# Slot lists loaded apart from their adding, expert weights put behind them, and writes of out without waits on one another

## The chip, the cores and the metric

One Trainium2 chip, of which the kernel uses one core. The metric is the device time of an execution in microseconds. The engines: PE (TensorE, matrix products and transposes), ACT (ScalarE), DVE (VectorE), POOL (GpSimd), and SP (SyncE), which here only issues DMAs and loads registers. Each engine works through its own stream in order and waits on semaphores. DMAs issued by SP and those issued by POOL go through different queues.

## What is computed

An attention with a window of 128, a mixing stage (two Fourier transforms, real part) with a dense feed-forward block, and a routed mixture of experts: 2304 tokens of 512 numbers, 8 experts with 1024 hidden units. The change touches only the last of the three. Cut to that:

```python
logits = np.einsum('bsd,de->bse', x, w_gate)
local_gate = 1.0 / (1.0 + np.exp(-np.einsum('bsd,de->bse', x, w_local).squeeze(-1)))
for b in range(B):
    prev_e = -1
    for s in range(S):
        fresh_e = int(np.argmax(logits[b, s]))
        if s == 0 or local_gate[b, s] < 0.5:
            e = fresh_e
        else:
            e = prev_e if prev_e >= 0 else fresh_e
        prev_e = e
        ls = logits[b, s] - logits[b, s].max()
        p = np.exp(ls)
        p /= p.sum() + 1e-09
        h = np.maximum(x[b, s] @ w1[e], 0.0)
        out[b, s] = p[e] * (h @ w2[e])
```

## The kernel before, in words

The dense block runs in two halves over nine groups of two 128-token tiles. While its second half runs, each finished group is routed: `route` makes logits and one-hot choices, `assign` turns them into a slot for each token (a running count for each expert) and scatters an entry (token, output row, factor) for each token into the DRAM lists `slots`, three lists whose sum is the entry. The experts are then taken in an order by their counts (`ranks`, `er` holds the expert of a rank and `eb` the first slot). The rows that a rank has room for are fixed: 224, 384, 320, 320, 296, 272, 232 and 216 for ranks 0 to 7. The two fullest tiles of the first expert are done early: rank -1, called the early FFN here, 256 rows, whose expert is known before the last groups are routed. Rank 0 is the same expert and uses the same weights.

A matrix product in full precision is three products of rounded halves: `split` (lines 164 to 166) makes the high half by a cast on ACT and the rest by a subtraction on DVE, and `mm3` (lines 168 to 171) issues the three matmuls. So every weight chunk of a rank (four chunks of 1 MB, each loaded by two DMAs from SP into a raw tile, of which there are two) costs four splits, and every tile of tokens four transposes on PE and a split (`transpose_split`, line 549).

`ffn` (line 563) is a generator. For each of 8 blocks f it issues 12 hidden matmuls, a relu on ACT and a second half of the relu on DVE, and yields; from f = 1 on it then issues the products with the second weights for block g = f - 1 (six matmuls for two tiles), and yields. So there are 16 yields, n = 0 to 15: n = 0 is f=0, n = 1 is f=1, then g=0, f=2, g=1, f=3 and so on to g=7. Between yields, other generators take steps: `beside` (inputs of the next rank), `soon` (the early expert) and `pre_` (weights). `last` holds the newest hidden matmul, relu and second half of a relu; `tc.issue_after(ins)` pins instructions behind one of them on its engine, and `behind()` (line 605) pins behind all three. What isn't pinned, the framework orders by itself: at build time it fills each engine's stream, in the order of the program as far as things are ready by its own estimate of times, else in another order. DMA issues on SP are ordered in the same way.

The inputs of a rank: `slot_load` (line 1118) loads the three lists, `slot_ids` (line 1124) adds them on DVE and copies the numbers out, `gather` (line 1100) fetches token rows by an indirect DMA from POOL (256 KB for a full tile), and `transpose_split` brings them into the form that the FFN reads. `early` (line 1137) does the same for the early FFN, in the dense block's last group: after the gathers it lets EY steps pass (5) and then transposes. `expert_inputs` (line 1212) does it for ranks 0 to 7, with `slot_load` and `slot_ids` in one step. In the early FFN (lines 1229 to 1240), at n = 5, expert 1's weights are queued first, then rank 0's inputs. `emit` (line 1106) scales a finished tile on ACT (or ACT and DVE) and writes its rows to `out` by an indirect DMA from POOL. Since each write may touch any row of `out`, the framework lets it wait for the one before.

## Time and profile before

| what | value |
|---|---|
| median of 3 runs | 980.01 us (977.08 to 980.98) |
| the profiled execution, its own time | 980.93 us |
| its span | 978.9 us |
| PE busy | 910.6 us (93%) |
| DVE, ACT, POOL busy | 521.8, 369.8, 239.7 us |
| early FFN | from 697.1 us on |
| FFN of rank 0 | from 736.2 us on |
| last matmul | 962.7 us |

The profiled execution is one of the program on the chip, taken by the hardware profiler. Its time lies 2.0 us above its span and 0.9 us above the median. Times in rows count from the span's start. In a timeline a row is: start, duration (both us), engine, line, operation, output<-input, shapes and a count, and in brackets how long the engine stood idle before it and what released it. A matmul's duration overlaps with the next; the distance of starts tells its cost. A line can be that of a helper: L169 to L171 are the three matmuls of `mm3`, L165 and L166 the two halves of `split`, L552 the transposes, L580 and L583 the relu and its second half. The name `hps` is a hidden block's result, `acc` the output's, `tps` a transposed tile, `we` raw weights, `xg` gathered rows, `ids` the lists, `idn` the slot numbers, `yo` a finished tile.

### The profile page before, as it was taken

How to read it: one execution, taken by the hardware profiler on the slowest of the kernel's cores; microseconds unless marked ns; L12 is line 12 of the kernel's file. 1: busy time of each engine (PE TensorE's matmuls, PEld its weight loads, DVE VectorE, ACT ScalarE, POOL GpSimd, SP SyncE). 2: the span in 40 equal slices, each digit the busy share in tenths (PEclk: the TensorE clock that was granted, in tenths of full speed). 3: DMA queues.
4: the chain of work that ended last, by engine and by line, in shares of the span. 5: the costliest groups of instructions: out<-in, count | busy, mean ns of one | idle time of the engine just before them, and what ended most of it. 6: DMA issues, size and time to landing. Idle time of an engine off the chain costs nothing. (4 is left out here: it accounts for less than half of the span.)

```text
span 978.9 us, 16130 instructions
## 1 busy us (share of the span) xinstructions
PE 910.6 (93%) x5878; PEld 752.2 (77%) x5879; DVE 521.8 (53%) x1332; ACT 369.8 (38%) x974; POOL 239.7 (24%) x364
## 2 busy tenths in 40 slices
PE   8868899989999999999999999998979999999993
PEld 4535677667778797889888888887758899988782
DVE  5787866745554658521333435357546545565410
ACT  5635363543553246421111111114235445455410
POOL 2315441231221137310111313123023211222100
PEclk9989799979999999999999999999988999999997
DMA  9923071341312396253444342536167555455100
GB/s 324 378 86 108 1 238 61 121 130 52 114 66 69 120 313 194 65 151 65 108 108 108 85 110 44 120 85 194 57 188 247 186 162 164 165 189 196 64 20 20
DMA packets 109036, 129.14 MB, mean 132 GB/s; under 512 B 16222, under 2 KB 78046, under 8 KB 108884
## 3 DMA queue, kind: packets, MB, share of 16 engines
q1 hardware_dynamic: 83636, 103.95, 33.3%
q0 software_dynamic: 22720, 19.36, 9.1%
q10 hardware_dynamic: 2592, 4.72, 1.3%
q8 instruction: 48, 0.79, 0.3%
q14 instruction: 40, 0.33, 0.1%
HBM read 99.65 MB, written 30.87 MB: 133 GB/s over the span
## 5 line engine op out<-in xcount | busy, mean ns | idle before, releaser
L580 ACT ACTIVATE h<-hps 128x256 fp32r<-128x256 f32 x152 | 58.2, 383 | 262.3 <-PE hps L171 259.0
L583 DVE SCALAR_TENSOR_TENSOR h<-hps,h 128x256 fp32r<-128x256 f32 x152 | 63.8, 420 | 160.0 <-ACT h L580 160.0
L169 PE MATMUL acc<-t,h 128*128 128x512 f32 x304 | 125.8, 416 | 3.0 <-ACT h L580 3.0
L171 PE MATMUL acc<-t,h 128*128 128x512 f32 x304 | 121.7, 400 | 1.5 <-DVE h L583 1.2
L170 PE MATMUL acc<-t,h 128*128 128x512 f32 x304 | 121.9, 401 | 1.0 <-POOL t L166 0.9
L166 DVE TENSOR_TENSOR t<-we,t 128x512 fp32r<-128x512 f32 x128 | 84.5, 694 | 46.9 <-ACT t L165 46.9
L169 PE MATMUL hps<-xT,t 128*128 128x256 f32 x288 | 87.0, 302 | 4.8 <-ACT t L165 3.5
L165 ACT CAST t<-we 128x512 fp32r<-128x512 f32 x128 | 73.4, 618 | 42.4 <-DMA we<-in_w 17.9
L171 PE MATMUL hps<-xT,t 128*128 128x256 f32 x288 | 84.7, 294 | 3.5 <-POOL t L166 3.5
L169 PE MATMUL hps<-xTe,t 128*128 128x320 f32 (+7 forms) x288 | 86.4, 301 | 0.6 <-ACT xTe L165 0.6
L170 PE MATMUL hps<-xTe,t 128*128 128x320 f32 (+7 forms) x288 | 86.0, 299 | 0.0
L171 PE MATMUL hps<-xTe,t 128*128 128x320 f32 (+7 forms) x288 | 85.8, 298 | 0.0
L170 PE MATMUL hps<-xT,t 128*128 128x256 f32 x288 | 83.9, 291 | 0.0
L169 PE MATMUL hps<-xTb,t 128*128 128x256 f32 x288 | 83.6, 290 | 0.0
L170 PE MATMUL hps<-xTb,t 128*128 128x256 f32 x288 | 82.3, 286 | 0.0
L171 PE MATMUL hps<-xTb,t 128*128 128x256 f32 x288 | 82.3, 286 | 0.0
L378 ACT ACTIVATE t<-t,mx 128x128 f32<-128x128 f32 (+1 forms) x160 | 62.6, 393 | 45.7 <-DVE mx L371 41.3
L171 PEld LDWEIGHTS acc<-t,h 128*128 128x128 f32 x304 | 57.8, 190 | 17.9 <-DVE h L583 5.0
L169 PEld LDWEIGHTS acc<-t,h 128*128 128x128 f32 x304 | 58.1, 192 | 14.8 <-ACT h L580 3.2
L169 PEld LDWEIGHTS hps<-xT,t 128*128 128x128 f32 x288 | 56.8, 197 | 12.5 <-ACT t L165 4.4
L170 PEld LDWEIGHTS acc<-t,h 128*128 128x128 f32 x304 | 58.2, 191 | 9.8 <-POOL t L166 2.8
L583 DVE SCALAR_TENSOR_TENSOR hE<-hps,hE 128x256 fp32r<-128x256 f32 (+4 forms) x96 | 30.8, 349 | 62.6 <-ACT hE L580 62.1
(280 smaller groups left out, 2018.3 us busy)
## 6 DMA issues: line engine op xcount, KB each, us to landing
we<-in_w SPq DMA_DIRECT2D x64, 512.0 KB
rw<-in_w_ch SPq DMA_DIRECT2D x32, 512.0 KB
qkt<-in_qk SPq DMA_DIRECT2D x15, 642.0 KB
nd<-xT SPq DMA_DIRECT2D x18, 512.0 KB
xTb<-nd POOLq DMA_DIRECT2D x18, 512.0 KB, 6.8
vt<-in_v SPq DMA_DIRECT2D x16, 384.0 KB
pd<-y ACTq DMA_DIRECT2D x18, 256.0 KB
ub<-ud SPq DMA_DIRECT2D x18, 256.0 KB
```

What stands on the lines that cost most here:

```text
L165: nc.scalar.copy(hi, src)
L166: (eng or nc.vector).tensor_tensor(out=lo, in0=src, in1=hi.bitcast(F32), op=ALU.subtract)
L169: nc.tensor.matmul(o, lhsT=wh, rhs=xh, start=start, stop=False, **kw)
L170: nc.tensor.matmul(o, lhsT=wh, rhs=xl, start=False, stop=False, **kw)
L171: return nc.tensor.matmul(o, lhsT=wl, rhs=xh, start=False, stop=stop, **kw)
L378: nc.scalar.activation(t[0:m, j], t[0:m, j], AF.Exp, bias=mx[0:m, j:j + 1], scale=-1.0, accum_out=sums[0:m, j:j + 1])
L580: last["relu"] = nc.scalar.activation(h[:, 0:n], hps[:, 0:n], AF.Relu)
L583: last["rest"] = nc.vector.scalar_tensor_tensor(out=h[:, lo:lo + c1 - c0], in0=hps[:, c0:c1], scalar=0.0, in1=h[:, c0:c1].bitcast(F32), op ...
```

## The change

Four things are changed.

1. EY is 7 instead of 5: the early expert's transposes come two steps later.
2. `expert_inputs` issues the list loads, lets `apart` steps pass (5 for rank 0, 3 for the others), and only then adds the lists, behind the newest relu. Its transposes are pinned behind the newest hidden matmul. In the loop over ranks, its first step comes at n = 0 instead of n = 2, and ahead of the weights' step.
3. In the early FFN rank 0's inputs are queued first. Expert 1's weights follow once the gathers are issued: two raw chunks are loaded behind the last list load on SP, and all splits happen in rank 0's FFN, behind its relus. Behind the early FFN's last hidden block stand 12 matmuls (128x512) whose result nobody reads; rank 0's last transposes are pinned behind them.
4. A write of `out` is declared independent of the write before it, except in the block for overfull experts (`single`), which isn't entered here.

```diff
-EY = 5
+EY = 7
 EL = 7
+IL = 5
+SPIN = 12
...
-    def expert_weights(r, e):
+    def expert_weights(r, e, ahead=False):
...
-        for c in range(F // CB):
-            t1, t2 = chunksE[r][c]
+        def raw(c):
             x = act.tile([P, 2, 4 * CB], F32, tag="xT", name="we")
             x1, x2 = x[:, 0].rearrange("p (k f) -> p k f", k=4), x[:, 1].rearrange("p (k f) -> p k f", k=per)
             nc.sync.dma_start(out=x1.unsqueeze(1), in_=w1[:, bass.ds(e, 1), :, c * CB:(c + 1) * CB])
             nc.sync.dma_start(out=x2.unsqueeze(1), in_=w2[:, bass.ds(e, 1), c * per:(c + 1) * per, :])
+            return x1, x2
+
+        q = []
+        if ahead:
+            with tc.issue_after(last["ids"].ins):
+                q = [raw(0), raw(1)]
+            yield
+        for c in range(F // CB):
+            t1, t2 = chunksE[r][c]
+            x1, x2 = q.pop(0) if q else raw(c)
...
-    def emit(acc, idx, m=P, both=False):
+    def emit(acc, idx, m=P, both=False, alone=True):
...
+        if alone and wrote:
+            tc.declare_no_dep(w.ins, wrote[-1], reason="each token has one slot, so the rows are others")
+        wrote.append(w.ins)
...
-            nc.sync.dma_start(out=x[:, i, 0:nt], in_=slots[i][bass.ds(s0, nt * P)].rearrange("(t p) c -> p t c", p=P))
+            last["ids"] = nc.sync.dma_start(out=x[:, i, 0:nt], in_=slots[i][bass.ds(s0, nt * P)].rearrange("(t p) c -> p t c", p=P))
...
-    def expert_inputs(r):
+    def expert_inputs(r, apart):
         nt = -(-CAPS[r] // P)
-        ids[r] = slot_entries(eb[r], nt, NL)
+        x = slot_load(eb[r], nt, NL)
+        for _ in range(apart):
+            yield
+        with behind():
+            ids[r] = slot_ids(x, nt, NL)
...
         for t in range(nt):
-            transpose_split(xTs[r], t * P, gs[t], rows[t])
+            with tc.issue_after(last["ffn"].ins):
+                transpose_split(xTs[r], t * P, gs[t], rows[t])
             yield
...
-            pre_.add(expert_weights(1, er[1]))
-            pre_.step()
-            beside.add(expert_inputs(0))
-            beside.step(TE)
-        elif xp is not None and n < 15:
-            pre_.step(2)
+            beside.add(expert_inputs(0, IL))
+            beside.step()
+            left = IL + TM - 1
+        elif xp is not None and left:
+            left -= 1
+            beside.step()
+            if not left:
+                pre_.add(expert_weights(1, er[1], True))
+                pre_.step()
+    spin = ps_a2.tile([P, DM], F32, tag="acc2", name="spin")
+    t2 = chunksE[-1][0][1]
+    with behind():
+        for _ in range(SPIN):
+            last["ffn"] = nc.tensor.matmul(spin, lhsT=t2[:, 0, 0, 0:P], rhs=t2[:, 0, 0], start=True, stop=True)
...
-            beside.add(expert_inputs(r + 1))
+            beside.add(expert_inputs(r + 1, 3))
...
-            pre_.step(1 if r else 2)
-            if n >= 2:
-                beside.step()
+            beside.step()
+            with behind() if r == 0 else nullcontext():
+                pre_.step(1 if r else 2)
```

## Rows read from the trace of the kernel before

**Rows 1.** Busy time by stretch: PE, PEld, DVE, ACT, POOL; PE clock; DMA share; GB/s

```profile
730.00:740.00 10.00, 6.08 (x28) 5.22 (x29) 6.82 (x15) 6.74 (x13) 2.18 (x3) 0.62 0.86 249
```

**Rows 2.** PE's timeline at the early expert's transposes

```profile
687.70 0.78 PE L552 MATMUL tps<-ident,xg 128*128 128x128 f32 x4 [1.93 <-DMA xg<-x2d,idn]
...
690.83 0.90 PE L552 MATMUL tps<-ident,xg 128*128 128x128 f32 x4
...
692.97 0.28 PE L169 MATMUL hps<-xTb,t 128*128 128x256 f32 x1
...
694.39 0.40 PE L169 MATMUL acc<-t,h 128*128 128x512 f32 x1
```

**Rows 3.** PE's timeline from the early FFN to that of rank 0

```profile
721.36 0.28 PE L171 MATMUL hps<-xTe,t 128*128 128x256 f32 x1
724.67 0.50 PE L169 MATMUL acc<-t,h 128*128 128x512 f32 x1 [3.02 <-ACT h L580]
...
730.75 0.65 PE L552 MATMUL tps<-ident,xg 128*128 128x128 f32 x4 [1.72 <-DMA xg<-x2d,idn]
...
734.70 0.90 PE L552 MATMUL tps<-ident,xg 96*128 96x96 f32 x4 [2.60 <-DMA xg<-x2d,idn]
736.17 0.77 PE L169 MATMUL hps<-xTe,t 128*128 128x224 f32 x2 [0.57 <-ACT xTe L165]
...
743.48 0.26 PE L169 MATMUL hps<-xTe,t 128*128 128x224 f32 x1
...
744.81 0.40 PE L169 MATMUL acc<-t,hE 128*128 128x512 f32 x1
...
746.21 0.26 PE L169 MATMUL hps<-xTe,t 128*128 128x224 f32 x1
```

**Rows 4.** Timelines of DVE and of PE in rank 1's FFN

```profile
766.25 0.38 DVE L1128 TENSOR_TENSOR ids<-ids 128x12 f32<-128x12 f32 x2 [4.10 <-DMA ids<-slots]
...
768.66 0.50 PE L171 MATMUL acc<-t,hE 128*128 128x512 f32 x1 [1.31 <-DVE hE L583]
```

**Rows 5.** POOL's timeline behind the last matmul

```profile
963.45 1.00 POOL L1115 DMA_INDIRECT out<-yo,idn  x1 [17.20 <-ACT yo L1114]
967.50 1.00 POOL L1115 DMA_INDIRECT out<-yo,idn  x1 [3.06 <-issue]
```

**Rows 6.** POOL's timeline at the seam, and all gathers of line 1103 to landing

```profile
713.16 0.98 POOL L990 DMA_INDIRECT slots<-ent,su  x1 [0.30 <-issue]
726.48 1.35 POOL L1103 DMA_INDIRECT xg<-x2d,idn  x1 [12.34 <-ACT h L580]
728.14 1.18 POOL L1103 DMA_INDIRECT xg<-x2d,idn  x1 [0.31 <-issue]
...
DMA to landing us min/median/max: 4.4/5.1/6.5
```

**Rows 7.** Timelines of ACT and of DVE at the seam

```profile
721.56 1.14 ACT L165 CAST t<-we 128x512 fp32r<-128x512 f32 x2 [5.10 <-DMA we<-in_w]
...
725.61 0.16 DVE L1131 COPY idn<-ids 128x2 f32<-128x2 f32 x1
```

**Rows 8.** SP's DMA issues by line, 700 to 720: min/median/max ns, first to last start

```profile
L1089 SPq DMA_DIRECT2D we<-in_w x2: 372/382/393, 715.0 to 718.9; - x2
...
L1121 SPq DMA_DIRECT2D ids<-slots x3: 373/745/792, 715.6 to 717.2; - x3
```

**Rows 9.** Instructions of POOL's queue behind the last matmul, by line: min/median/max ns, starts

```profile
L1115 POOLq EVENT_SEMAPHORE  x1: 3386/3386/3386, 963.3 to 963.3; - x1
...
L1292 POOLq EVENT_SEMAPHORE  x5: 17/43/43, 970.4 to 970.8; - x5
```

**Rows 10.** Timelines of PE and of DVE in rank 2's FFN (320 rows)

```profile
806.10 0.39 PE L169 MATMUL acc<-t,hE 128*128 128x512 f32 x1
806.77 0.56 DVE L583 SCALAR_TENSOR_TENSOR hE<-hps,hE 128x256 fp32r<-128x256 f32 x2 [1.79 <-ACT hE L580]
...
809.70 0.60 PE L552 MATMUL tps<-ident,xg 128*128 128x128 f32 x4
```

More of the change, by code (lines that the diff above doesn't have):

```diff
@@ L1104, in gather @@
         return g
-    def emit(acc, idx, m=P, both=False):
+    wrote = []
+    def emit(acc, idx, m=P, both=False, alone=True):
         y = act.tile([P, DM], F32, tag="y", name="yo")
@@ L1114, in emit @@
             nc.scalar.activation(y[0:m], acc[0:m], AF.Copy, scale=idx[0:m, 2:3].bitcast(F32))
-        nc.gpsimd.indirect_dma_start(out=out, out_offset=IOA(ap=idx[0:m, 1:2], axis=0), in_=y[0:m], in_offset=None,
-                                     bounds_check=NT - 1, oob_is_err=False)
+        w = nc.gpsimd.indirect_dma_start(out=out, out_offset=IOA(ap=idx[0:m, 1:2], axis=0), in_=y[0:m], in_offset=None,
+                                         bounds_check=NT - 1, oob_is_err=False)
+        if alone and wrote:
+            tc.declare_no_dep(w.ins, wrote[-1], reason="each token has one slot, so the rows are others")
+        wrote.append(w.ins)
     def slot_load(s0, nt, lists):
@@ L1265, in single @@
                 mm3(acc, t[:, 0, f, 0:P], t[:, 1, f, 0:P], t2[:, 0, f % per], t2[:, 1, f % per], c + f == 0, c == 2 and f == 3)
-        emit(acc, idx)
+        emit(acc, idx, alone=False)
     nc.vector.tensor_single_scalar(eid[:, 0], eid[:, 0], 3, op=ALU.arith_shift_right)
```

## The prediction

> **What bounds the kernel now.** The page comes first: of the engines TensorE is busy longest by far, so a change can only pay where PE stands idle or runs at the lower clock, or behind its last matmul. The table by stretch finds the largest such place: from 730 to 740 PE is busy for 6.08 us of 10 at a granted clock of 0.62, between its two levels of 1.2 and 2.4 GHz, while the DMA engines are 0.86 busy [rows 1]. PE's timeline then names what it waits for. First, at 687.70 the early expert's first transpose waits 1.93 us for a gather, and the hidden block behind it runs at half clock until 690.83 [rows 2]. Second, the seam between the early FFN and the FFN of rank 0: from the last hidden matmul at 721.36 to the third hidden block at 743.48 there are four large waits (3.02 for a relu, 1.72 and 2.60 for gathers, 0.57 for the split after them) and two stretches at half clock [rows 3]. Third, 1.31 us at 768.66 [rows 4]. Fourth, the tail behind the last matmul, where the second write of out starts 4.05 us after the first [rows 5].
>
> The chain that makes the seam is read backwards over four engines. The gathers start at 726.48 and 728.14 [rows 6], because the slot numbers were ready at 725.77 [rows 7]; those wait for lists issued from 715.6 to 717.2, behind the first raw weights at 715.0 [rows 8]. ScalarE meanwhile sits in its in-order stream at a cast that waits for those weights until 721.56 [rows 7], and the relu behind it holds PE (the 3.02 us). So one early load, that of expert 1, is late for ACT and in the way of the lists at once.
>
> **EY from 5 to 7.** The two early transposes move behind one more acc block and one more hidden block. From 685.6 on that is hidden f=6 (1.42 us at full clock, the distance of 692.97 and 694.39 [rows 2]), acc g=5 (1.40 [rows 3]), then the first transpose at 688.4, after the landing seen at 687.70. The second follows at 690.2; that its gather has landed by then isn't seen, only that it has at 690.83 without a wait. The wait of 1.93 goes, and of the 3.13 us from 687.70 to 690.83 about 1.35 (0.36 for the transposes and 1.42 would do). Together 3.3, less 0 to 0.6 if the second gather is late: I take 3.2. The split of the second tile (some 1.3 us) ends before the early FFN starts at some 693.8, so nothing else becomes late.
>
> **The seam: IL, the weights put behind the lists, the spin.** All times here are 3.2 us earlier than in the trace. The lists depend on the last scatter into slots (713.16, now 710.0). The last of the three list loads was issued at 717.2 [rows 8], some 4 us after that scatter; now that is 714.0. How long a list takes with no weights ahead of it the trace doesn't show. Bounds: 3.3 us, by a write of out that starts at 963.45 and whose successor's wait ends at 966.7 [rows 5, 9], and some 8 us, by the same list behind a megabyte (717.2 to the slot numbers of 725.6, less the adds) [rows 7, 8]. I take 3.3, as the change puts it ahead. Slot numbers need 0.7 us on DVE (0.38 for two adds [rows 4], 0.16 for each of two copies [rows 7]) and are pinned behind the relu of f=5, which is past by then. POOL starts 0.2 to 0.7 later (725.77 to 726.48 [rows 6, 7]). First gather near 718.2, second 1.7 later at 719.9; landing 4.4 to 6.5, median 5.1 [rows 6]: second tile there at 724.3 to 726.4, say 725.1. PE ends f=7 at 718.3, and g=6 and g=7 at 721.1, as nothing stands ahead of the relus any more: the casts of expert 1's weights are pinned behind the relus of the next FFN. Twelve spin matmuls of 0.233 (1.40 for six [rows 3]) last until 723.9. They cost nothing as long as the gathers are later than that, and 2.8 us if these came at once. The transposes then wait 1.2, the split takes 1.3 more, and the FFN starts at 726.4. Before, it started at 736.17, and its first 7.31 us (to 743.48) would have taken 4.06 at full clock (two hidden blocks of 1.33 and one acc block of 1.40 [rows 3]), so the equal start is 739.4. Gain 13.0, of which 3.2 were counted: 9.8. The last idle stretch may again drop the clock, as the 1.93 us did [rows 2], at 1.35 us there and 3.25 at the seam (7.31 less 4.06); I put 0.8 on it. **Seam 9.0**, bounds 5 (gathers of 6.5 us and the clock lost) and 11.
>
> **Expert 1's weights inside rank 0's FFN.** Two raw chunks (2 MB) are issued behind the lists, two more when buffers come free. The 16 splits put 9 us on ACT (1.14 for two [rows 7]) and about as much on DVE, in an FFN of some 23 us (eight times 2.73 [rows 3], and transposes). Raws 3 and 4 leave at about 731 and 735, land some 6.5 us later (715.0 to 721.56 [rows 7, 8]) and are split by 745, 4 us before rank 1 starts and needs the first of them. The cover is that slack; without it PE would wait up to 3 us. I take 0.5. SP moves no more DMAs than before, only in another order, so later ranks start with their weights one half rank less ahead, which their length hides (28.8 us at 320 rows, eight times the 3.60 of [rows 10]).
>
> **Lists of ranks 1 to 7.** In rank 1's FFN, DVE stood 4.10 us at a list add with the relu's second half behind it, and PE lost 1.31 [rows 4]. With the add three steps after the load and behind a relu this goes: 1.3.
> But the pin has a price. Now slot numbers and gathers run almost a whole FFN ahead; then they start only after the third hidden block's relu. Take the FFN of 320 rows [rows 10]: that block ends at 806.10 (call it X), DVE starts the relu's second half at 806.77 and ends 0.56 later, the slot numbers take 0.7, POOL's start 0.2 to 0.7: the gather starts at X + 2.1 to 2.6 and lands at X + 6.5 to 9.1. The transposes stood at 809.70, after g=1 and f=3 (3.60 us); one step later, behind g=2 as well, that is X + 5.5. So **PE waits there 1.0 us by the quickest landing, 2.2 by the median and the later start, 3.6 by the slowest**; nothing of it is in the trace of before. In rank 0's FFN the place by the program is X + 4.1, in rank 1's about X + 6.3, in the last two, with two tiles, X + 3. But the order isn't only the program's. In the seam the transposes stood inside g=7, far behind their place in the program (f=3), and the slot numbers behind the relu of f=6; between lie g=5, f=7, g=6 and half of g=7, 4.8 us by [rows 3], less 1.2 for that relu. So the framework reckons some 3.6 us from slot numbers to landing, which puts the transposes at X + 5.2 or later everywhere. Bounds for seven FFNs: 0 (transposes placed later still) and 25. I take the quickest landing, **1.0 each, 7.0 in all**, because the DMA engines are less full later than in the seam.
>
> **Writes of out.** POOL no longer waits for a landing. In the middle nothing waits for POOL. In the tail the second write can start 0.3 after the first ends, at 964.75 instead of 967.50; the semaphores that close the kernel stand behind it on POOL's queue, at 970.4 to 970.8 [rows 9], and move with it; the other engines' stand earlier. **2.75**, bounds 0 and 3.
>
> Sum: 3.2 + 9.0 + 1.3 + 2.75 - 0.5 - 7.0 = 8.75. The profiled execution took 980.93 us, 2.0 more than its span; 972.2 by the sum. The median of the three runs is 0.9 below that execution, so I predict **971.3**, by itself 966 to 976.
>
> **Rivals.**
> *Gathers in time* (0.26): the transposes are placed late enough and none of the seven waits. For it: no such wait is in the trace after rank 0; against it: that trace gathers far ahead. Time 964.3.
> The Trainium skill would have it so: "DMA: Bandwidth & Descriptors", section "Anatomy of one DMA — SWDGE (gpsimd) path", puts a DMA from GpSimd at 2.0 us and its bytes over 436 GB/s, which for 256 KB is 2.6 us (an estimate). The landings of 4.4 to 6.5 us disagree, and they decide.
> *Seam half won* (0.18): the two raw megabytes behind the lists slow the lists and gathers (one gather took 6.5 us beside such weights), the clock falls again, or casts in rank 0's FFN wait for raws 3 and 4. The seam gives 4, the rest as summed: 976.3.
> *Slower* (0.12): the pinned slot numbers make every gather late enough to idle PE and drop its clock. At a landing of 6.5 us the seven waits are 21 to 25 us, and half clock behind them, as the 1.35 us after the 1.93 us wait, adds about 8: some 993. It decides from 2.3 us per FFN, which is a landing of 5.7 us with the gather at X + 2.1; the median is 5.1.
> The forecast itself has 0.44.
>
> **How the numbers follow.** Measurement of this kernel can tell about 0.5% from no change. Below 975.1 lie the first rival, most of the forecast and a third of the third case: 0.70. Within 0.5%: 0.18. Above 984.9: 0.12. The range leaves out a little of the first rival and most of the slower one: 962 to 982.
>
> **What would show it.** Right: PE's 1.93, 3.02, 1.72 and 2.60 waits gone; lists ahead of raw weights on SP; twelve spin matmuls before rank 0; the last two writes of out 1.3 us apart. The forecast's own mark is a wait of PE at the transposes for gathers, about 1 us, in each FFN from rank 0 on. No such row means 964; rows of 2 us and more with a clock below 1.00 mean no gain. Wrong altogether: ACT or DVE standing at casts in rank 0's FFN with PE behind them.

## The result, and the profile after

The changed kernel takes 996.23 us in the median of four runs (993.01 to 999.53), beside 980.50 for the kernel before in the same comparison (977.08 to 984.08). The ratio is 1.0141, 95% interval 1.0099 to 1.0182. A gain of 9 us was forecast; it is a loss of 14 to 16. Of three kernels further down, one or two runs take over 1.5% longer than that kernel's fastest; the ratios leave these out, the medians don't. The profiled execution took 995.45 us with a span of 993.3, 14.4 more than before.

The first look is again the page: PE is busy 919.4 us, 8.8 more than before, for the same matmuls and the twelve new ones. Matmuls at half clock count double, so the loss isn't only waiting. DVE, ACT and POOL are busy as long as they were, to some 3 us.

```profile
PE 919.4 (93%) x5891; PEld 757.4 (76%) x5891; DVE 523.9 (53%) x1332; ACT 370.4 (37%) x974; POOL 242.9 (24%) x364
```

Next, PE's timeline gives the start of each FFN (its first hidden matmul), and with them five stretches that add up to the span. This table, in us, is what the rest goes by; "forecast" is the sum of the prediction, laid out on the same stretches (9.8 for the earlier start of rank 0; then 0.5 and 1.0 less the clock's 2.45; then six times 1.0 less 1.3; then 2.75).

| stretch | before | after | change | forecast |
|---|---|---|---|---|
| up to the early FFN | 697.1 | 695.4 | -1.8 | |
| early FFN, to the start of rank 0 | 39.0 | 33.3 | -5.7 | -9.8 with the row above |
| FFN of rank 0 | 26.4 | 37.4 | +11.0 | -0.95 |
| FFNs of ranks 1 to 7 | 200.6 | 213.0 | +12.4 | +4.7 |
| behind the last matmul | 15.8 | 14.2 | -1.55 | -2.75 |
| span | 978.9 | 993.3 | +14.4 | -8.8 |

So what was meant to gain did gain, and two stretches lose 23.4 us. PE's timeline at the early transposes and the seam, to be held against [rows 2, 3]:

```profile
690.34 0.60 PE L554 MATMUL tps<-ident,xg 128*128 128x128 f32 x4
...
692.20 0.60 PE L554 MATMUL tps<-ident,xg 128*128 128x128 f32 x4
...
722.48 2.88 PE L1270 MATMUL spin<-t 128*128 128x512 f32 x12
727.00 1.15 PE L554 MATMUL tps<-ident,xg 128*128 128x128 f32 x8 [1.64 <-DMA xg<-x2d,idn]
728.72 0.48 PE L171 MATMUL hps<-xTe,t 128*128 128x224 f32 x2 [0.57 <-ACT xTe L167]
...
746.96 1.12 PE L554 MATMUL tps<-ident,xg 128*128 128x128 f32 x4 [4.86 <-DMA xg<-x2d,idn]
...
758.50 0.50 PE L171 MATMUL acc<-t,hE 128*128 128x512 f32 x1 [0.39 <-ACT hE L582]
...
762.73 0.50 PE L171 MATMUL acc<-t,hE 128*128 128x512 f32 x1 [0.93 <-ACT hE L582]
```

The waits of 1.93, 3.02, 1.72 and 2.60 us are gone; 1.64 is left, at a place where PE had spun. New is the wait of 4.86 us inside rank 0's FFN, for tiles of rank 1. The table by stretch (columns as in [rows 1]) shows the clock behind both waits:

```profile
730.00:740.00 10.00, 10.00 (x54) 9.12 (x54) 6.14 (x13) 5.19 (x11) 0.00 (x0) 0.70 0.21 65
740.00:750.00 10.00, 5.14 (x28) 4.45 (x26) 5.21 (x11) 4.19 (x8) 3.41 (x3) 0.81 0.99 325
750.00:760.00 10.00, 9.57 (x52) 7.81 (x52) 6.88 (x12) 6.09 (x13) 0.00 (x0) 0.85 0.49 166
```

From 730 to 740 PE never rests, but the granted clock is 0.70, and the DMA engines are at 0.21: until 736.80 both raw tiles are full, and nothing is on the way. From 740 to 750 they are at 0.99 and PE is busy half the time.

The chain that ended last (start, us, what) now leads over gathers in nearly every FFN:

```profile
719.45 7.50 DMA xg<-x2d,idn
740.63 6.29 DMA xg<-x2d,idn
756.62 4.64 DMA we<-in_w
769.65 7.15 issue
779.84 6.74 DMA xg<-x2d,idn
812.71 6.45 DMA xg<-x2d,idn
845.68 5.54 DMA xg<-x2d,idn
878.35 5.99 DMA xg<-x2d,idn
...
907.18 5.46 DMA xg<-x2d,idn
```

and the list of waits from 760 on (total us, times, longest) has a row that has no counterpart before:

```profile
PE tps L554 <- DMA xg<-x2d,idn: 9.7, 9, 2.4
```

### The profile page after: what moved, and what is told of

The parts are those of the page before. It is cut to its first block, busy times and chain, and to the rows that moved or that the text cites. A ratio compares the mean times of both kernels' runs of the same rounds, so it can differ in the third digit from the quotient of the medians.

```text
span 993.3 us, 16135 instructions
## 1 busy us (share of the span) xinstructions
PE 919.4 (93%) x5891; PEld 757.4 (76%) x5891; DVE 523.9 (53%) x1332; ACT 370.4 (37%) x974; POOL 242.9 (24%) x364
## 3 DMA queue, kind: packets, MB, share of 16 engines
q1 hardware_dynamic: 83636, 103.95, 32.4%
## 4 chain that ended last, share of the span: by engine, by line
PE 63%; DVE 14%; issue 9%; DMA 7%; ACT 3%; POOL 3%; SPq 0%; POOLq 0%; DVEq 0%; ACTq 0%
PE hps L171 8%; PE hps L173 8%; PE hps L172 8%; PE acc L171 7%; PE acc L173 7%; PE acc L172 7%; DMA xg<-x2d,idn 4%; PE o L408 3%; PE s L365 3%; PE tps L554 2%; PE zps L496 2%; PE pt L389 1%; ACT t L167 1%; PE acc L599 1%; DVE t L269 1%
## 5 line engine op out<-in xcount | busy, mean ns | idle before, releaser
L171 PE MATMUL hps<-xTe,t 128*128 128x320 f32 (+7 forms) x288 | 87.6, 305 | 0.6 <-ACT xTe L167 0.6
L172 PE MATMUL hps<-xTe,t 128*128 128x320 f32 (+7 forms) x288 | 86.9, 302 | 0.3 <-DVE xTe L168 0.3
L173 PE MATMUL hps<-xTe,t 128*128 128x320 f32 (+7 forms) x288 | 86.9, 302 | 0.0
```

Of the source, the lines that this page charges most:

```text
L171: nc.tensor.matmul(o, lhsT=wh, rhs=xh, start=start, stop=False, **kw)
L172: nc.tensor.matmul(o, lhsT=wh, rhs=xl, start=False, stop=False, **kw)
L173: return nc.tensor.matmul(o, lhsT=wl, rhs=xh, start=False, stop=stop, **kw)
```

## The experiments

All stretches in this table are from one profiled execution each, in us; the ratio is that of the timed runs to the kernel before, run beside them, with its 95% interval. Compare ratios, not medians: the kernel before itself has medians from 978.35 to 982.34 in these comparisons. The part of the profile ahead of the early FFN differs by several us between executions of the same code there (below), which is why the stretches stand apart.

| kernel | early FFN starts | early FFN | rank 0 | ranks 1-7 | end | median | ratio |
|---|---|---|---|---|---|---|---|
| e1_ey | 693.5 | 38.7 | 25.3 | 202.2 | 15.8 | 977.96 | 0.9980 (0.9958-1.0003) |
| e2_writes | 691.8 | 39.0 | 25.4 | 202.3 | 13.9 | 975.99 | 0.9963 (0.9941-0.9985) |
| e3_seam | 694.9 | 33.7 | 39.9 | 203.7 | 13.6 | 987.97 | 1.0105 (1.0062-1.0148) |
| e4_lists | 694.5 | 38.4 | 31.1 | 225.0 | 15.8 | 1004.23 | 1.0232 (1.0188-1.0276) |
| e5_ey_writes | 694.4 | 37.5 | 25.1 | 202.0 | 14.6 | 975.97 | 0.9960 (0.9926-0.9993) |
| e6_free | 697.5 | 36.1 | 28.6 | 202.7 | 14.1 | 979.71 | 1.0010 (0.9973-1.0048) |
| e7_gap | 697.9 | 36.1 | 32.4 | 201.4 | 13.8 | 979.25 | 0.9984 (0.9949-1.0019) |
| e8_lists_writes | 697.0 | 38.7 | 29.7 | 209.6 | 14.9 | 991.55 | 1.0106 (1.0048-1.0165) |
| e9_later | 700.4 | 33.6 | 37.2 | 199.4 | 15.0 | 983.82 | 1.0020 (0.9986-1.0055) |
| e10_gap4 | 693.1 | 33.8 | 28.0 | 202.2 | 14.4 | 977.20 | 0.9935 (0.9901-0.9970) |
| e11_gap4_spin | 696.6 | 34.2 | 26.8 | 207.5 | 13.9 | 980.11 | 0.9962 (0.9924-0.9999) |
| e12_both | 693.1 | 34.2 | 28.1 | 205.9 | 14.6 | 975.52 | 0.9934 (0.9900-0.9968) |
| e13_old_seam | 691.4 | 38.6 | 25.4 | 199.7 | 13.8 | 976.65 | 0.9969 (0.9931-1.0007) |

### The parts, one by one

**EY alone**, in the kernel before:

```diff
-EY = 5
+EY = 7
```

> The kernel before with EY = 7 and nothing else. In the changed kernel the two early transposes no longer wait, and from 683.46 to 697.14 (13.68 us) of before became 9.99 us, 3.7 less; yet the early FFN started only 1.76 us earlier there. Theory 1 (EY's gain is real, and what took part of it back, the 1.76 us wait of PE at 670.68 for the relu's second half, comes with EY's other order of work in the last dense group): 1.5 to 2.5 us faster than before, with that wait in the trace at about 670. Theory 2 (that wait belongs to the other parts of the change, as the lists and their order): about 3.5 us faster, no wait at 670. Theory 3 (the seam behind it takes the gain back, since rank 0's gathers end when they end): within 0.7 us of before, with rank 0's FFN starting at about 736 as before.

977.96 beside 979.87 us. The early transposes don't wait (688.45 and 690.32). PE has no wait for a relu near 670; it has one of 1.73 for ACT at 671.32, in the routing of the last groups. So the size is theory 1's, though the interval (0.9958 to 1.0003) holds no change and theory 2's 3.5 us too; but its reason falls: the wait for the relu's second half isn't EY's (of the eleven kernels with EY at 7 the changed one and e5_ey_writes have it at 1.76 and 1.88 us, the others at 0.41 or less). Theory 3 falls too: rank 0 starts at 732.1, its tiles come earlier with the rest. A second view bears the size out. There is a transpose ahead of the early FFN that waits about 0.61 us for DVE in all fifteen traces (at 649.42 in before). From it to the early FFN, which is where EY acts, it takes 45.5 to 49.3 us in the four kernels with EY at 5 (mean 47.4), and 44.6 to 46.2 in the eleven with EY at 7 (mean 45.3): 2.1 us. In one of the four, e2_writes, the transposes didn't wait even with EY at 5, because PE had stood 2.86 us for DVE at 674.48.

**Independent writes alone**, in the kernel before:

```diff
-        nc.gpsimd.indirect_dma_start(out=out, ...)
+        w = nc.gpsimd.indirect_dma_start(out=out, ...)
+        if alone and wrote:
+            tc.declare_no_dep(w.ins, wrote[-1], reason="each token has one slot, so the rows are others")
+        wrote.append(w.ins)
```

> The kernel before with the writes of out independent of one another and nothing else. The forecast put 2.75 us on this, from the second write starting 1.3 us after the first. In the changed kernel the two did start 1.3 us apart, but the time from the last matmul to the span's end fell by 1.55 us only (15.76 to 14.21). Theory 1 (the last landing, which the closing waits for, ends the kernel, so only part of the earlier start comes back): 1.3 to 1.8 us faster. Theory 2 (the forecast's term is right and something else lengthened the changed kernel's tail): 2.5 to 3 us faster.

The stretch behind the last matmul falls from 15.8 to 13.9; over the twelve kernels with independent writes it is 14.2 in the mean, over the three without 15.8. Theory 1: 1.5 us. The timed gain of 3.9 us is larger, but its interval reaches down to 1.5. Where the rest of the 2.75 went stands in POOL's timeline of after, and in the list of its queue's instructions at the kernel's end (line 1322: min/median/max ns, starts), to be held against [rows 5, 9]:

```profile
979.39 1.01 POOL L1129 DMA_INDIRECT out<-yo,idn  x1 [19.45 <-ACT yo L1128]
980.71 1.02 POOL L1129 DMA_INDIRECT out<-yo,idn  x1 [0.30 <-DVEq L1322]
```

```profile
L1322 POOLq EVENT_SEMAPHORE  x5: 17/42/1329, 983.5 to 985.2; - x5
```

The second write starts 1.3 us after the first, as forecast. But one of the five closing semaphores now takes 1.33 us, where the longest was 0.04: the wait for the landing has moved from the second write to the end.

**The seam alone**: the changed kernel with the inputs of ranks 1 to 7 as before.

```diff
-            beside.add(expert_inputs(r + 1, 3))
+            beside.add(expert_inputs1(r + 1))   # lists and adds in one step, nothing pinned, as before
...
-            beside.step()
             with behind() if r == 0 else nullcontext():
                 pre_.step(1 if r else 2)
+            if n >= 2:
+                beside.step()
```

> The changed kernel, with the inputs of ranks 1 to 7 as before: lists loaded and added in one step, slot numbers and transposes not pinned, their first step from n = 2 on and behind the weights' step. EY, the seam of rank 0 with expert 1's weights behind the lists, the spin and the independent writes all stay. Theory 1 (the pinned slot numbers make the gathers late, so that PE waits at the transposes and runs at half clock behind them: 11.0 us in rank 0's FFN and some 12 in the others): 972 to 978, and no wait of PE for gathers of over 0.5 us behind rank 0's first block. Theory 2 (expert 1's weights, split in rank 0's FFN behind its relus, with casts on ACT that wait for late raw weights, are the loss): rank 0's FFN keeps over 33 us of its 37.39, and the time stays at 984 or above.

987.97: slower than before by 1.05%, and rank 0's FFN takes 39.9 us. Its one wait for a gather is 2.53 us at 731.89, where an unpinned transpose of rank 1 stands in the first block. For rank 0 theory 2 holds, for ranks 1 to 7 (203.7) theory 1. SP's, ACT's and PE's timelines of this kernel show how:

```profile
716.32 0.37 SPq L1090 DMA_DIRECT2D we<-in_w  x1
...
717.60 0.37 SPq L1090 DMA_DIRECT2D we<-in_w  x1
...
738.68 0.37 SPq L1090 DMA_DIRECT2D we<-in_w  x1
...
741.41 0.37 SPq L1090 DMA_DIRECT2D we<-in_w  x1
...
747.88 0.37 SPq L1090 DMA_DIRECT2D we<-in_w  x1
```

```profile
734.93 0.36 ACT L582 ACTIVATE hE<-hps 128x224 fp32r<-128x224 f32 x1 [6.40 <-PE hps L173]
735.19 1.13 ACT L167 CAST t<-we 128x512 fp32r<-128x512 f32 x2
...
751.53 1.14 ACT L167 CAST t<-we 128x512 fp32r<-128x512 f32 x2 [2.64 <-DMA we<-in_w]
752.58 0.35 ACT L582 ACTIVATE hE<-hps 128x224 fp32r<-128x224 f32 x1
...
758.71 1.14 ACT L167 CAST t<-we 128x512 fp32r<-128x512 f32 x2 [3.23 <-DMA we<-in_w]
759.75 0.35 ACT L582 ACTIVATE hE<-hps 128x224 fp32r<-128x224 f32 x1
```

```profile
752.98 0.80 PE L171 MATMUL acc<-t,hE 128*128 128x512 f32 x1 [3.75 <-ACT hE L582]
...
760.16 0.79 PE L171 MATMUL acc<-t,hE 128*128 128x512 f32 x1 [2.88 <-ACT hE L582]
```

Two raw chunks leave at 716 and 718. Their casts are pinned behind rank 0's first relu, which is at 734.93. There are only two raw tiles, so the third chunk doesn't leave before 738.68; ACT had stood idle for 6.40 us ahead of that relu. From there each chunk is late, among them those of expert 2, whose casts the framework has put ahead of rank 0's relus: ACT stops at a cast, the relu stands behind it, and PE behind the relu.

**The pinned lists alone**, in the kernel before:

```diff
-            beside.add(expert_inputs(r + 1))
+            beside.add(expert_inputs1(r + 1, 3))   # as in the change: adds three steps on, pinned
...
+            beside.step()
             pre_.step(1 if r else 2)
-            if n >= 2:
-                beside.step()
```

> The kernel before, with the inputs of ranks 1 to 7 alone as in the changed kernel: lists loaded at n = 0, added three steps later behind the relu, transposes pinned behind the newest hidden matmul. Early FFN, seam, weights and writes stay as before. Theory 1 (pinned slot numbers are the loss): 10 to 18 us slower than before, with PE waits for gathers in most FFNs; in rank 0's FFN a wait of 3 to 5 us, since nothing there but the pin sets the gather's start. Theory 2 (the loss in rank 0's FFN is that of the expert 1 weights, and the waits elsewhere are small): at most 6 us slower, rank 0's FFN within 3 us of its 26.38.

1004.23, worse than the whole change, and by more than theory 1 said: ranks 1 to 7 take 225.0 us. POOL's timeline in rank 4's FFN, and PE's at the transposes that follow, show a thing that the prediction had ruled out:

```profile
872.33 1.01 POOL L1115 DMA_INDIRECT out<-yo,idn  x1 [2.40 <-ACT yo L1110]
879.45 0.94 POOL L1115 DMA_INDIRECT out<-yo,idn  x1 [6.11 <-DVE t L166]
...
880.69 1.12 POOL L1103 DMA_INDIRECT xg<-x2d,idn  x1 [0.17 <-issue]
```

```profile
885.17 1.11 PE L552 MATMUL tps<-ident,xg 128*128 128x128 f32 x4 [4.21 <-DMA xg<-x2d,idn]
```

The slot numbers were ready at 877.19, but the gather stands on POOL behind the last write of out of rank 3, which waits 6.11 us. The releaser named (a split that had to do with neither) had long been done, so the wait is one for a landing; the next experiment takes it away.

**EY and writes together**, in the kernel before:

```diff
-EY = 5
+EY = 7
...
+            tc.declare_no_dep(w.ins, wrote[-1], reason="each token has one slot, so the rows are others")
```

> The kernel before with EY = 7 and the independent writes of out together. By themselves they took 1.9 us (ratio 0.998) and 3.9 us (0.9963). Theory 1 (one lies in the early FFN's inputs, the other behind the last matmul, so they add): 974 to 975, ratio 0.994. Theory 2 (EY's gain is given back at the seam, where rank 0's gathers end when they end; in its run the wait of PE for them was 3.91 us where before it was 1.72 and 2.60): 976, ratio 0.996, all of it from the writes.

975.97 beside 978.35 us. The interval of the ratio, 0.9926 to 0.9993, holds 0.994 as well as 0.996, so this doesn't tell the two apart. The stretches speak against a gain given back at the seam: early FFN and rank 0 take 62.7 us together, 64.3 with the writes alone.

### What the two losses are made of

**Pinned lists with independent writes**, the kernel above with the edit of e2_writes.

```diff
 # e4_lists, and
+        if alone and wrote:
+            tc.declare_no_dep(w.ins, wrote[-1], reason="each token has one slot, so the rows are others")
```

> The kernel of the fourth run (the kernel before with the pinned lists and transposes of ranks 1 to 7), with independent writes of out added. In the fourth run rank 4's last write of out waited 6.11 us on POOL for the landing of the write before it, and the three gathers stood behind it; PE waited 4.21 us there. In the changed kernel the gathers of the same rank started 1.9 us behind the end of the third hidden block. Theory 1 (the pin puts the gathers behind the previous rank's writes in POOL's queue, and a write's wait for a landing holds them): the FFNs of ranks 2 to 5 fall by 2 to 4 us each, 988 to 993 in all, over 10 us less than the fourth run. Theory 2 (the gathers are late by their own place behind the relu and by the DMA engines): only the tail's gain, 1 to 4 us less than the fourth run, 1000 or more.

Theory 1: ranks 1 to 7 fall from 225.0 to 209.6, the whole to 991.55. The same place on POOL's timeline:

```profile
869.70 2.17 POOL L1117 DMA_INDIRECT out<-yo,idn  x1 [2.32 <-DVE yo L1114]
...
873.39 1.01 POOL L1103 DMA_INDIRECT xg<-x2d,idn  x1 [1.40 <-DVE idn L1136]
```

No write waits for another, and the gather starts when its numbers are there. So beside pinned lists the writes are worth some 12 us by the ratios (1.0232 and 1.0106): they mend most of what the pin breaks. What is left, 8.7 us of waits for gathers from 760 on (18.0 without independent writes), is the distance of landing and transposes.

**Transposes two steps later**, in the changed kernel:

```diff
             gs.append(gather(ids[r][:, t], rows[t]))
             yield
+        for _ in range(2 if r else 0):
+            yield
```

> The changed kernel, with two more steps (one hidden and one acc block) between the last gather and the first transpose of ranks 1 to 7. Lists, pins, weights, seam, spin and writes as in the changed kernel. Theory 1 (the loss of ranks 1 to 7 is only that the transposes stand some 5.4 us behind the third hidden block and the tiles land some 8 us behind it): no wait of PE for gathers behind rank 0's own, the stretch from rank 1's FFN to the last matmul falls from 213.0 to 202 to 205 us; rank 0's FFN keeps 33 us or more, since its casts for late raw weights stay; 984 to 988 in all. Theory 2 (the pinned adds and transposes cost by their order on DVE and PE as well): the waits go, but that stretch stays at 208 or more, 991 or more in all.

Theory 1: no wait of PE for a gather from 760 on, ranks 1 to 7 in 199.4 us, 13.6 less than in the changed kernel and 1.2 less than before (the list adds that held DVE in [rows 4] don't any more). The whole is 983.82, since rank 0's FFN stays at 37.2. There one wait for a gather of 1.46 is left (4.86 in the changed kernel) and the stretch is 0.2 shorter: with the tiles in time, PE waits 2.86, 1.12, 0.78 and 0.55 for relus instead. PE's timeline there:

```profile
751.39 0.66 PE L554 MATMUL tps<-ident,xg 128*128 128x128 f32 x4 [1.46 <-DMA xg<-x2d,idn]
...
756.67 0.50 PE L171 MATMUL acc<-t,hE 128*128 128x512 f32 x1 [2.86 <-ACT hE L582]
```

So in rank 0's FFN the raw weights set the time, and the wait for gathers hid it.

**The splits in other places.** First without the pin in rank 0's FFN, then with eight splits behind the early FFN's last relu, both in the kernel of e3_seam:

```diff
# e6_free
-            with behind() if r == 0 else nullcontext():
-                pre_.step(1 if r else 2)
+            pre_.step(1 if r else 2)
# e7_gap
+    with behind():
+        pre_.step(8)
     for t, x in enumerate(acc):
         emit(x, ids[-1][:, t])
```

> The kernel of the third run (the changed one with the inputs of ranks 1 to 7 as before), where in rank 0's FFN the splits of expert 1's weights are no longer pinned behind its relus, so that the framework may place them into the early FFN's end. In the third run ACT and DVE stood idle from 721.5 to 727.5 with both raw chunks on the way, the splits came from 735 on, the next two raw chunks left only at 738.7 and 741.4, and three relus of rank 0 stood behind casts waiting for raw weights (3.83, 2.64 and 3.23 us). Theory 1 (the pin is what makes the later raws late): rank 0's FFN below 30 us, a relu of the early FFN late by 1 to 3 us again, 976 to 981 in all. Theory 2 (loads that leave behind the lists are late by themselves): rank 0's FFN over 35 us, 984 or more.

> The kernel of the third run, with the eight splits of the first two raw chunks of expert 1 placed behind the early FFN's last relu, in the stretch in which PE spins, ahead of rank 0's first split. Theory 1 (the pin behind rank 0's relus makes the later raws late): the next two raw chunks leave by 729 and land by 737, rank 0's FFN takes 26 to 29 us, 974 to 978 in all, with no relu of the early FFN delayed. Theory 2 (what holds rank 0 is DMA time: the first two raws, the lists of rank 1 and the gathers all go through full DMA engines from 717 to 726, and the next raws then meet the gathers of rank 1): PE still waits for relus behind casts in rank 0's FFN, which stays over 33 us, 982 or more.

979.71 and 979.25; by the ratios that is 9 and 12 us less than e3_seam. In e6_free it went as theory 1 has it: rank 0 takes 28.6, 11.3 less than in e3_seam (with the same kind of wait for a tile of rank 1, 3.29 at 737.34), and the early FFN 2.4 more, since casts of the first chunks stand ahead of a relu there (1.78 at 725.16) and ahead of rank 0's first split (2.94 at 733.57). e7_gap lies between its theories, with rank 0 at 32.4: the second chunk's casts hold rank 0's first split (2.92 at 734.01), and a cast of expert 2 holds a relu of rank 0 (2.22 at 748.85).

**Four splits in the gap, and expert 2's behind rank 1's relus**, in e3_seam; then the same with a longer spin:

```diff
# e10_gap4
+    with behind():
+        pre_.step(4)
     for t, x in enumerate(acc):
         emit(x, ids[-1][:, t])
...
-            with behind() if r == 0 else nullcontext():
+            with behind() if r <= 1 else nullcontext():
# e11_gap4_spin, besides
-SPIN = 12
+SPIN = 24
```

> The kernel of the third run (inputs of ranks 1 to 7 as before), with the four splits of the first raw chunk of expert 1 placed behind the early FFN's last relu, the second chunk's behind rank 0's first relu, and the splits of expert 2's weights pinned behind rank 1's relus. In the run with eight splits there, rank 0's first split waited 2.92 us behind casts of the second chunk, and a relu of rank 0 stood behind a cast of expert 2 whose raw weights had left at 743.8 and were waited for until 747.4. Theory 1 (these two orders on ACT are what rank 0 still loses): early FFN to rank 1's FFN takes 58 to 61 us (65.4 before, 68.6 with eight splits, 62.7 for the kernel with EY and writes alone), 970 to 974 in all. Theory 2 (raw chunks and gathers share full DMA engines, so something is late in any order): 64 us or more there, 977 or more.

> The kernel before this one with 24 spin matmuls in place of 12, so that PE is busy until about the landing of the second gather. In the changed kernel the spin ended 1.64 us before the gathers, and the first three blocks of rank 0 took 7.75 us at a granted clock of 0.50 to 0.70 instead of 4.06. Theory 1 (the idle 1.64 us and the 0.57 behind it drop the clock, and PE kept busy keeps it): those blocks take under 5 us, and 1 to 3 us less in all than with 12. Theory 2 (PE's wait for the split of the tiles, or the transposes themselves, drop it anyhow): the blocks stay at 7 us or more, and the time is the same or up to 2 us longer.

e10_gap4 is the first that lies more than 0.5% below the kernel before, 977.20 beside 982.34 us (e2_writes and e5_ey_writes have intervals below 1 too, at 0.4%); early FFN and rank 0 take 61.8 us together, 65.4 before and 70.7 in the changed kernel. That is just above theory 1's 58 to 61; the whole time is at theory 2's 977. Two orders were changed at once here, and which of them gained was not tried. PE's timeline at the seam of e10_gap4, and busy time and clock from 725 on:

```profile
720.13 2.88 PE L1283 MATMUL spin<-t 128*128 128x512 f32 x12
725.15 1.12 PE L554 MATMUL tps<-ident,xg 128*128 128x128 f32 x8 [2.14 <-DMA xg<-x2d,idn]
```

```profile
725.00:730.00 5.00, 3.92 (x21) 3.40 (x22) 1.16 (x2) 0.97 (x2) 0.00 (x0) 0.74 0.89 271
730.00:735.00 5.00, 5.00 (x22) 4.40 (x22) 3.96 (x11) 3.63 (x8) 3.34 (x3) 0.58 0.34 84
```

The same two views of e11_gap4_spin:

```profile
723.70 5.61 PE L1283 MATMUL spin<-t 128*128 128x512 f32 x24
729.15 0.93 PE L554 MATMUL tps<-ident,xg 128*128 128x128 f32 x8
```

```profile
725.00:730.00 5.00, 5.00 (x27) 4.10 (x26) 0.34 (x1) 0.91 (x3) 2.01 (x2) 1.00 1.03 285
730.00:735.00 5.00, 3.91 (x28) 3.22 (x28) 2.25 (x8) 2.61 (x7) 0.31 (x1) 1.00 0.59 182
```

With 24 the clock stays at its upper level, and rank 0's first three blocks take 5.07 us (730.80 to 735.87) instead of 7.83 (726.87 to 734.70), although PE still stands 0.72 and 0.33 us at the split. Theory 1 holds for these blocks: 2.8 us less there, 0.4 lost by starting later. But rank 0's FFN as a whole is only 1.2 shorter (26.75 beside 27.95); further on in it PE waits 1.38 at 749.67 for a relu's second half, where e10_gap4 waits 0.79. In all the gain wasn't seen: ranks 1 to 7 took 207.5 us in this execution, with a wait of PE of 2.97 at 833.35, where DVE stood 3.42 at an unpinned list add, the stall of [rows 4] once more.

### Two versions with both steps mended

e12_both is the changed kernel with the edits of e9_later, e10_gap4 and e11_gap4_spin. e13_old_seam is the kernel before with EY at 7, independent writes, and the pinned lists with the later transposes; its seam is that of before.

```diff
 # e12_both: the changed kernel, and
+        for _ in range(2 if r else 0):
+            yield
...
-SPIN = 12
+SPIN = 24
...
+    with behind():
+        pre_.step(4)
...
-            with behind() if r == 0 else nullcontext():
+            with behind() if r <= 1 else nullcontext():
 # e13_old_seam: e8_lists_writes, and
-EY = 5
+EY = 7
...
+        for _ in range(2 if r else 0):
+            yield
```

> The changed kernel with its two losing steps mended: transposes of ranks 1 to 7 two steps later, four splits of expert 1's first chunk behind the early FFN's last relu, expert 2's splits pinned behind rank 1's relus, 24 spin matmuls. Theory 1 (the two losses were the late gathers and the late raw weights, and the parts are otherwise worth what they were forecast to be, EY and writes and the list adds off the path): early FFN to rank 1 61 to 63 us, ranks 1 to 7 199 to 201, 968 to 973 in all, ratio 0.988 to 0.993. Theory 2 (pinned gathers in rank 0's and rank 1's FFN meet the raw weights that now leave there, so tiles or casts are late again): 975 or more.

> The kernel before with EY = 7, independent writes, and the pinned lists of ranks 1 to 7 with transposes two steps later; the seam (expert 1's weights ahead of rank 0's lists, no spin) as before. Theory 1 (the new seam is worth some 2 us by itself once its order on ACT is mended): ranks 1 to 7 199 to 201 us, early FFN to rank 1 62 to 65, 972 to 975 in all, 2 to 4 us behind the kernel sent with it. Theory 2 (the seam is worth nothing, since rank 0's tiles land when they land): within 1 us of that kernel.

e12_both: 975.52 beside 980.87 us, ratio 0.9934; it and e10_gap4 have the lowest ratios, with intervals that overlap those of e2_writes and e5_ey_writes. Its seam is as expected (62.3 us), although in rank 0's FFN PE waits 2.87 us at 743.34 and 0.98 at 746.31 for tiles of rank 1. Ranks 1 to 7 aren't as expected (205.9): in rank 2's FFN PE waits 2.00 us for a gather that started at 803.88 and landed 5.85 later. Theory 2 has these waits, and the whole time (975 or more). That expert 2's raw chunks, moved half a rank on, meet that gather, is likely (the DMA engines are 0.93 busy from 800 to 810) but wasn't tried. e13_old_seam has ranks 1 to 7 at 199.7, as e9_later. The two differ by 1.1 us in their medians and by 3.4 by their ratios, with intervals that overlap; what the new seam is worth by itself stays open.

## Why the prediction was wrong

The span is 23.2 us longer than the sum had it: 2.3 of that stand ahead of rank 0's FFN, 12.0 in it, 7.7 in the FFNs of ranks 1 to 7, and 1.2 behind the last matmul.

The waits that the change was meant to remove went, as forecast, and gave less than it said. **EY** was put at 3.2; it is worth about 2. Of the four kernels with EY at 5, three wait for the gather (1.93, 1.69 and 1.69 us) and e2_writes doesn't, and only two run the next hidden block at half clock (in e8_lists_writes the second transpose comes 1.90 us after the first, in the kernel before 3.13).

**The seam's earlier start** was put at 9.8 with EY and came to 7.45. Of the missing 2.3, the later start of the early FFN is 1.4 (695.38, where the sum had 693.9). The gathers started at 719.45 and 720.75, 0.2 and 0.6 earlier than forecast from that start, but the first took 7.5 us to land, not 5.1; that is about half of the rest, and transposes and split, 1.7 us instead of 1.3, are the other half.

**The clock** was the mis-sized term of that step: 0.8 was put on it, and the first three blocks of rank 0 took 7.75 us where 4.06 was full clock, 3.7 more, after an idle time of 1.64 and 0.57 us. In e11_gap4_spin and e12_both, where 24 matmuls leave no wait between spin and transposes, these blocks take 5.07 and 4.76 us at a granted clock of 1.00; so here the gap between the two is what costs it. Earlier start and clock together gave 7.0 (the start that full clock would need for the same third block moves from 739.4 to 732.4). Less the 1.8 by which the early FFN starts earlier, 5.2 are left for the seam, just above its lower bound of 5.

**The stall of DVE** in [rows 4] went. **The tail** gave 1.5 of 2.75, as the landing is now waited for at the end.

Two steps failed. The first is **expert 1's weights inside rank 0's FFN**, "I take 0.5", bound 3. e6_free against e3_seam, which differ in the pin of the splits alone, puts 11.3 us on it in rank 0 and some 9 in all; e12_both against e9_later, where the order of the splits and the spin differ, takes rank 0 from 37.2 to 28.1. The sum had the third chunk leave at 731 and the fourth at 735; they left at 736.80 and 740.30. ACT's and SP's timelines of the changed kernel:

```profile
732.24 0.36 ACT L582 ACTIVATE hE<-hps 128x224 fp32r<-128x224 f32 x1 [3.58 <-PE hps L173]
```

```profile
736.80 0.37 SPq L1090 DMA_DIRECT2D we<-in_w  x1
```

Rank 0 began 2.3 us later than forecast, its first hidden block ran at half clock, so its relu came at 732.24, and only the four splits behind that relu set a raw tile free. And the step counted how long the splits take on ACT (9 us of 23), not what stands behind them there: a cast whose chunk hasn't landed holds every relu behind it. The last sentence of the prediction's marks, ACT standing at casts in rank 0's FFN with PE behind them, is what e3_seam (3.75 and 2.88 us) and e9_later (2.86) show. In the changed kernel the wait for the gather covers most of it, and PE waits 0.39 and 0.93 for relus. That mark had no price among the rivals, only a clause in "Seam half won". Of the 11.0 us that rank 0's FFN grew by, 6.7 are idle time of PE and 4.3 are matmuls at the lower clock.

The second is **the lists of ranks 1 to 7**, seven waits of 1.0; the waits for gathers came to 14.6 us, 4.86 in rank 0's FFN and 9.7 behind it. The prediction saw the price of the pin. With X for the end of the third hidden block, it worked out the landing at X + 6.5 to 9.1 and the transposes' place by the program at X + 4.1 in rank 0's FFN. In the changed kernel X is 737.80 there, the gather started at 740.63 and landed at 746.92, X + 9.1; PE stood ready for it at 742.10, X + 4.3. So in that FFN the upper end of the landing was right. The framework was supposed to hold the transposes back by 3.6 us from the slot numbers, read off one place where they stood late; it placed them by the program. This step isn't apart from the first: the gather ran beside late raw weights, with the DMA engines at 0.99 from 740 to 750. In e8_lists_writes, with the pin and the old seam, the waits of that FFN are 0.85, 1.23 and 0.65.

In the FFNs of ranks 1 to 6 the quickest landing was no bad choice for the first tile. Where PE waited for that tile (ranks 2, 5 and 6) it could go on 3.4 to 3.6 us after the gather's start, and these waits are 3.7 of the 9.7 us. The other 6.0 are waits for the second and third tiles, which the sum had left out: their gathers start some 1.3 us behind one another, and those on the chain above take 5.5 to 6.7 us to land. "Less full later" holds for a rank's mean (the DMA engines were 0.45 to 0.59 busy over the FFNs of ranks 1 to 5) and not for these gathers, during which they were 0.68 to 0.89 busy. For rank 2's FFN, first gather and second (columns as in [rows 1]):

```profile
811.40:814.98 3.58, 3.09 (x17) 2.44 (x16) 3.06 (x6) 2.15 (x5) 2.97 (x3) 1.00 0.46 139
812.71:819.16 6.45, 4.16 (x24) 3.28 (x22) 3.23 (x8) 2.49 (x5) 2.19 (x2) 1.00 0.80 249
```

The Trainium skill, "DMA: Bandwidth & Descriptors", section "Anatomy of one DMA — SWDGE (gpsimd) path", would give 2.6 us for 256 KB by its fit (an estimate); the landings here, 3.4 to 7.5 us, disagree.

**"In the middle nothing waits for POOL"** was true of the kernel before and false of the changed one without its writes: there the gathers ran almost a rank ahead of the writes of out, and the pin put them behind. e4_lists against e8_lists_writes puts some 12 us on it. The change escapes this because its fourth part mends what its second breaks; the forecast had costed both parts by themselves.

Of the rivals, "Seam half won" has all three of its conditions in the trace (the gather of 7.5 us beside the raw weights, the clock, the casts); its 4 us for the seam is near the 5.2 found, but it left the rest as summed. "Slower" named the mechanism of the second step and 993 us, from seven waits of 3 to 3.6 us and half clock behind them. The time was near, but not for that reason: the waits in the six FFNs behind rank 0 were 9.7 us in all, the granted clock over ranks 1 to 7 was 0.99, and about half of the loss is rank 0's FFN, where the weights set the time.

## What to carry to other kernels

When work is pinned behind an engine's later instruction, follow the buffers as well as the engine: the next load leaves when the last reader of its tile is done, and from there count to the instruction in whose in-order stream the late data will be waited for. When a step moves, list what stands ahead of it on each queue at its new place, and cost parts that share a queue together. A gather's distance to its use is laid out by the slowest landing that the trace shows, not the quickest, and for the last tile of a rank, not the first.

## What the runs showed of the hardware

An indirect gather from POOL lands 5.5 to 7.5 us after its start on the chain of the changed kernel, with the DMA engines between 0.68 busy and full meanwhile. One of these has 16 rows only (32 KB, at 878.35) and takes 5.99 us behind two full ones. The first gathers of ranks 2, 5 and 6, of 256 KB, let PE go on after 3.4 to 3.6 us, with the DMA engines 0.34 to 0.46 busy. POOL's own row for such a gather is 1.00 us (at 740.63, where the chain has 6.29 to the landing). The Trainium skill, "Perfetto Trace Analysis", section "DMA Instruction — SWDGE (GPSIMD)", says that such a row ends when the last descriptor is made and not when the data has moved; these two numbers agree. An idle time of PE of 2.2 us in two pieces was followed by a granted clock of 0.50 from 730 to 735 in the changed kernel, the lower of its two levels (1.2 of 2.4 GHz); idle times of 0.72 and 0.33 were not (1.00 in e11_gap4_spin). Nor were a wait of 2.87 at 743.34 in e12_both (1.00 from 743 to 750) and one of 2.35 at 942.56 in the changed kernel (1.00 from 942 to 948), so the runs don't show which idle times cost the clock and which don't. A write that waits for another write's landing holds everything behind it on POOL, 6.11 us in e4_lists. And executions differ ahead of the change: the early FFN started between 691.4 and 700.4 us in the fifteen profiles, with EY accounting for some 2 us of it, so that an effect of 2 us is read from a stretch, not from the end.
